# A fused attention kernel whose first batch is reordered: products ahead of masks, smaller array tiles, a shorter decoding

## The chip, the cores and the metric

The kernel runs on one core of one Trainium2 chip. The metric is the device time of the program in microseconds (us). The core's engines work side by side, each in the order of its own instructions: TensorE (PE for its products, PEld for its loads of stationary operands), VectorE (DVE), ScalarE (ACT), GpSimd (POOL) and SyncE (SP), which here only issues DMAs. They meet through semaphores alone, so an instruction that waits holds back everything behind it on its own engine.

## The reference

Two blocks follow each other. The first is a polynomial attention without softmax: queries and keys (4 batches, 4 heads, 1088 positions, 32 numbers) are turned into 64 features each, as products of two 8-number sketches. The second is a mixture of four causal attention experts, of which every position uses two.

```python
def phi(x):                                   # S1, S2: 8 x 32
    a = einsum('rd,bhsd->bhsr', S1, x);  b = einsum('rd,bhsd->bhsr', S2, x)
    return einsum('bhsi,bhsj->bhsij', a, b).reshape(..., 64)
kv  = einsum('bhsf,bhsd->bhfd', phi(k), v);   z = sum(phi(k), axis=2)
x   = einsum('bhsf,bhfd->bhsd', phi(q), kv) / (einsum('bhsf,bhf->bhs', phi(q), z) + 1e-6)
x   = x as (batch, 1088, 4 heads * 32 = 128)
logits = x @ w_gate                           # 4 experts
topk   = the two largest;  w = softmax over these two
for e in range(4):
    scores = (x @ wq[e]) @ (x @ wk[e]).T / 8, causal
    ye     = softmax(scores) @ (x @ wv[e]) @ wo[e]
    out   += w[e] * ye   where e is one of the two of the position
```

## The kernel before

The positions of a batch are cut into nine tiles of 128 (the last holds 64). Since every position uses two of four experts, each tile has two "slots" instead of four experts. The work on a batch is cut into tasks, and all tasks of the four batches are written out in one list, `ORDER` (lines 22 to 40). A word such as `0.cu:4` means: batch 0, task `cu`, argument 4. `TASKS` (line 773) maps the names to functions, and a loop at the end calls them one after the other; each call appends instructions to the engines that it uses. So the list fixes the order on every engine, the DMA queue of SyncE included. Nothing is reordered later.

The tasks that matter here, in the order of one batch:

- `ld` (`load_next`): the DMAs of k, q and v of a batch into `kin`, `qin`, `vin`, each a single buffer. `bk` (`begin_k`) copies v into `vp` on GpSimd and transposes k into `kT` on VectorE; `bq` does q. For batch 0, `vk` copies v.
- `ks`, `qs` (`sketch`, and `first_sketch` for batch 0): TensorE multiplies with the sketch matrix, ScalarE copies, VectorE and GpSimd form the 64 features. The sketch matrix itself comes in as 64-bit numbers, which VectorE decodes into a leading and a trailing fp32 part (lines 197 to 235). `SKH` is its arrangement for batch 0, `SKW` for the others.
- `kv` (`kvs`): the sums over the keys, 9 tiles x 4 heads of products whose stationary operand is a head's 64 features, into `kvz`.
- `tf` turns q's features, `nu` (`numer`) multiplies them with `kvz` and divides; the result is `xs`. `tx` turns it into `xT`. `sw` saves `xs` to DRAM, and `sp` (`spread_x`) loads it again, arranged by keys in blocks of 32, into the four row groups of the single buffer `xrep`.
- `ga`, `ge`, `gw` (`gate`): logits, choice (`sel`) and weights. `md` sends the choice through DRAM to all partitions, as masks `mk`. Batch 0 does not wait for that: `mp` (`masks`) multiplies the choice with an identity on TensorE (line 543) and has ScalarE copy it out as 8-bit masks.
- `cu` (`chosen`): for two tiles, the queries times the four experts' matrices `mcat` (line 556), then ScalarE copies two of them and VectorE puts the other two in where the mask says so (`copy_predicated`, line 562). The result `uT` holds the chosen slots. `em` makes `mcat`, `eo` the matrices of the outputs.
- `s` (scores and softmax, lines 595, 570, 574), `t` (transposition of the weights into the store of their group, `aTB` or `aTA`), `vb` and `va` (values of the two groups, line 651), `shb`, `sha`, `shp` (shares), `zb` and `o` (outputs, lines 724 to 736).
- `warm` is a task of filler products on TensorE that compute nothing.

PSUM has eight banks, and the helper `bank(n)` hands out the least recently used one or aligned group. The masks for the causal rows (`mask`, `mask_back`, `mask_last`) and other constants are built by GpSimd ahead of all tasks (lines 172 to 195).

Of the kernel before, what the change touches and what calls it, by code (L numbers as in the profile page):

```python
# [10 lines left out]
F32 = mybir.dt.float32  # L11
# [11 lines left out]
    0.bk 0.bq1 0.bq0 0.ks:0:4 0.vk 0.ks:4:9 0.qs:4:9 0.qs:0:4 0.tf:13:18 0.kv 0.eo 1.ld 0.tf:8:13 1.bk 0.tf:0:8  # L23
    1.ks:4:9 1.ks:0:4 0.nu:0:4 0.warm:2 0.nu:4:9 0.sw 0.tx:0:4 0.warm:2 1.bq 2.ld 0.warm:2 0.warm:2 0.ga:0:4 0.tx:4:9
    0.ge:0 0.gw:0 1.kv 0.ga:4:9 1.qs:4:9 0.em 0.mp:2:4 0.mp:4:6 1.tf:8:13 1.tf:13:18 0.mp:0:2 0.ge:4 0.sp 0.mp:6:8
    2.bk 0.mp:8:9 1.qs:0:4 2.bq 3.ld 1.nu:5:9 0.cu:4 0.cu:6 0.cu:0 0.gw:4 1.tf:0:8 2.ks:4:9 0.cu:2 0.s:5:1 1.nu:0:5
    2.ks:0:4 0.s:3 0.md 0.s:4:2 0.t:3 1.tx:0:4 0.t:5 0.t:1 2.kv 0.shb 1.tx:4:9 2.qs:4:9 2.qs:0:4 0.cu:8 0.s:7 0.s:8
    0.t:2 2.tf:13:18 0.t:4 1.ga:0:9 1.md 0.t:7 0.s:6:0 0.t:8 0.t:0 0.vb:0 0.vb:1 0.vb:2 0.vb:3 1.ge:0 2.tf:8:13 0.zb:3
    1.sw 1.cu:0 0.t:6 1.cu:4 0.o:3 1.cu:2 1.cu:6 1.s:4:2 0.zb:5 1.s:5:1 1.s:3 0.va:0 0.sha 3.bk 0.va:1 0.va:2 1.t:4
    1.t:5 2.tf:0:8 1.t:2 3.ks:0:4 3.bq 0.va:3 1.sp 1.t:1 2.nu:0:5 0.o:5 0.zb:6 1.cu:8 1.s:7 0.o:6 0.zb:0 2.tx:0:4  # L30
    1.t:3 3.ks:4:9 2.nu:5:9 1.s:6:0 0.zb:1 0.o:0 2.tx:4:9 1.s:8 1.gw:0 1.shb 0.zb:8 3.kv 2.ga:0:9 2.ge:0 1.vb:0 2.md
    2.sw 0.o:8 1.t:7 1.vb:1 3.qs:4:9 1.t:8 3.qs:0:4 1.t:0 1.t:6 1.vb:2 1.vb:3 2.cu:4 2.cu:2 0.o:1 1.zb:5 2.cu:0
    2.s:4:2 2.s:5:1 3.tf:13:18 1.sha 1.zb:3 1.va:0 1.va:1 3.tf:8:13 2.t:4 2.cu:6 1.o:3 1.o:5 2.t:1 3.tf:0:8 2.gw:0
    1.va:2 1.zb:1 2.t:5 1.va:3 3.nu:5:9 2.sp 2.s:3 2.t:2 2.s:6:0 3.nu:0:5 1.o:1 2.shb 2.t:3 3.sw 3.tx:4:9 1.zb:8
    3.tx:0:4 2.s:7 2.t:0 2.cu:8 1.o:8 3.ga:0:9 1.zb:6 1.zb:0 3.md 2.t:7 2.vb:0 2.vb:1 2.s:8 2.vb:2 2.vb:3 1.o:0 3.ge:0
    2.t:6 2.t:8 3.cu:8 3.cu:2 3.cu:4 1.o:6 2.sha 3.cu:0 3.cu:6 3.s:4:2 2.zb:5 3.s:5:1 3.t:2 3.t:1 3.s:3 2.zb:1 3.t:4
    3.t:3 2.o:5 2.zb:3 2.va:0 2.va:1 3.t:5 2.va:2 2.va:3 3.sp 3.s:8 2.o:3 2.o:1 3.gw:0 3.shb 3.t:8 2.zb:0 2.zb:6 3.s:7
    3.s:6:0 3.t:6 2.o:6 2.o:0 3.t:7 3.vb:0 3.vb:1 3.vb:2 3.t:0 3.vb:3 3.zb:1 3.va:0 3.va:1 3.va:2 3.zb:3 3.o:3 3.o:1
    3.shp 3.zb:5 2.zb:8 3.va:3 3.o:5 3.zb:0 2.o:8 3.o:0 3.zb:6 0.warm:2 3.zb:8 3.o:6 3.o:8
# [4 lines left out]
def kernel(  # L44
# [65 lines left out]
    kvz = const("kvz", [128, 2, D + 1])  # L110
# [60 lines left out]
    identb = const("identb", [128, 128], BF16)  # L171
    make_identity(nc, ident)
# [7 lines left out]
    for t in (mask, mask_back, mask_last):  # L180
        nc.gpsimd.memset(t, 0.0)
    for out_, cols, base in ((mask[:, 896:], 128, 0), (mask_last[0:64], 64, 0), (mask_last[64:], 64, 0),
                             *((mask_back[32 * r : 32 * r + 32, 384:], 128, 96 - 32 * r) for r in range(4))):
        nc.gpsimd.affine_select(out=out_, in_=out_, compare_op=ALU.is_ge, fill=-1e30,
                                base=base, pattern=[[-1, cols]], channel_multiplier=1)
    lower = const("lower", [128, E, E])
    nc.gpsimd.memset(lower, 0.0)
    for e in range(1, E):
        nc.gpsimd.memset(lower[:, e, 0:e], 1.0)
    nc.gpsimd.memset(SKH, 0.0)  # L190
    nc.gpsimd.memset(SKW, 0.0)
# [5 lines left out]
    if NS == 2:  # L197
# [4 lines left out]
        lead, last, ok = (words[:, x].bitcast(F32) for x in range(4, 7))  # L202
# [10 lines left out]
        def both(o, x, y, op):  # L213
# [17 lines left out]
            out=last, in0=last, scalar=2.0**-52, in1=sg.bitcast(F32), op0=ALU.mult, op1=ALU.mult)  # L231
        both(lead, ma.bitcast(F32), ok, ALU.mult)
        both(S_hi, lead, last, ALU.add)
        both(lead, lead, S_hi, ALU.subtract)
        both(S_lo, lead, last, ALU.add)
# [6 lines left out]
    for h in range(H):  # L242
        nc.gpsimd.tensor_copy(SKW[32 * h : 32 * h + 32, :, :, h % 2, :],
                              ST[:, :, 0 : 2 * R].rearrange("d n (x r) -> d n x r", x=2))
# [44 lines left out]
    def spread_x(b):  # L289
        for r in range(4):  # L290
            nc.sync.dma_start(out=xrep[32 * r : 32 * r + 32], in_=saved[b].rearrange("(c k) d -> k c d", k=32))
# [15 lines left out]
    class Batch:  # L307
# [5 lines left out]
        def __init__(self, b):  # L313
            self.b, self.ab, self.fp, self.uT, self.mp = b, {}, {}, {}, None
            self.yT, self.qpT = yT, qpT
# [17 lines left out]
    def begin_k(b):  # L333
        if b:
            nc.gpsimd.tensor_copy(vp[:, 0 : NJ - 1, :, 0:D].rearrange("p j h d -> p h j d"), vin)
            nc.gpsimd.tensor_copy(vp[0:64, NJ - 1, :, 0:D], vtl)
        n = NJ - 1
        nc.vector.transpose(kT[:, 0 : 128 * n].rearrange("p (j g t) -> p j g t", j=n, g=4),
                            kin[:, 0 : 128 * n].rearrange("p (g j d) -> p j g d", g=4, j=n))
        nc.vector.transpose(kT[:, 128 * n : S], kin[:, 128 * n : S])  # L340
# [5 lines left out]

    def load_next(b):
        load_rows(kin, k, b)
        load_rows(qin, q, b)
        load_v(b)  # L350
# [5 lines left out]
    def first_sketch(nm, j0, j1):  # L356
# [60 lines left out]
    def kvs(b):  # L417
        kp, k0 = batch(b).fp["k"], bank()
        kv = P[:, k0, 0 : 2 * (D + 1)].rearrange("p (m d) -> p m d", m=2)
        for m in range(2):  # L420
            for j in range(NJ):
                for x in range(2):
                    h = 2 * m + x
                    nc.tensor.matmul(kv[64 * x : 64 * x + 64, m], kp[:, j, h], vp[:, j, h, :],  # L424
                                     start=(j == 0), stop=(j == NJ - 1))
        nc.scalar.copy(kvz, kv)
# [6 lines left out]
    def numer(b, x0, x1):  # L433
        k0, m, qpT = bank(2), 2 * (x1 - x0), batch(b).qpT
        for y in range(2 * x0, 2 * x1):
            c = (D + 1) * (y - 2 * x0)
            for x in range(2):
                for half in (0, 64):
                    rows = slice(64 * x, 64 * x + 64)
                    nc.tensor.matmul(P[half : half + 64, k0 + x, c : c + D + 1], qpT[rows, y, half : half + 64],  # L440
                                     kvz[rows, y % 2], start=True, stop=True)
        den = p2.tile([128, 2, 2 * NJ], F32, tag="den", name=f"den{b}_{x0}")[:, :, 0:m]
        nus = P[:, k0 : k0 + 2, 0 : m * (D + 1)].rearrange("p x (m d) -> p x m d", d=D + 1)
        nc.vector.tensor_scalar_add(den, nus[:, :, :, D], 1e-6)
        nc.vector.reciprocal(den, den)
        for x in range(2):
            nc.vector.tensor_tensor(
                out=xs[:, x0:x1].rearrange("p j (m x d) -> p x (j m) d", m=2, x=2)[:, x], in0=nus[:, x, :, 0:D],
                in1=den[:, x, :, None].to_broadcast([128, m, D]), op=ALU.mult)
# [84 lines left out]
    def masks(b, j0, j1):  # L534

        m_, k0 = batch(b), bank(2)
        if m_.mp is None:
            m_.mp = p2.tile([128, NJ, 4, 128], F8, tag="mk", name=f"mp{b}")
        sb = p2.tile([128, 2, 2 * X], BF16, tag="selb", name=f"selb{b}_{j0}")
        nc.vector.tensor_copy(sb[:, 0 : j1 - j0].rearrange("p j x -> p (j x)"), m_.sel[:, 2 * X * j0 : 2 * X * j1])  # L540
        for j in range(j0, j1):
            for n, x in enumerate((1, 2, 3, 4)):
                nc.tensor.matmul(P[:, k0 + j - j0, 128 * n : 128 * n + 128],
                                 sb[:, j - j0, x : x + 1].to_broadcast([128, 128]), identb, start=True, stop=True)
        nc.scalar.copy(m_.mp[:, j0:j1].rearrange("p j x q -> p (j x q)"), flat[:, 512 * k0 : 512 * (k0 + j1 - j0)], saturate=False)

    def chosen(b, i):

# [272 lines left out]
```

## Time and profile before

| | us |
|---|---|
| median of 3 runs | 286.47 |
| lowest, highest | 284.15, 287.38 |
| profiled execution | 287.48 |
| its span, first to last instruction | 285.7 |
| TensorE busy | 272.0 |
| VectorE busy | 220.4 |
| ScalarE busy | 105.2 |
| GpSimd busy | 59.3 |
| mean granted TensorE clock | 0.982 |

The page divides the span into 40 slices of 7.14 us; a digit gives the busy share of an engine in a slice in tenths, and the row PEclk the granted clock in the same way. A row of the timeline has start, duration, engine, line, operation and tiles, with the number of merged instructions after the x; the bracket names the idle time just before it and what ended it. The chain of work that ended last is followed back from the last instruction; a piece of it has start, duration, engine, tile, line and count. A product in fp32 shows as two instructions.

### The profile page before, as it was taken

The page shows a single profiled execution, that of the slowest core. Times are in us where ns is not written, and L with a number is a line of the kernel's source. Part 1 is how long each engine was busy: PE and PEld are TensorE (multiplying, and loading weights), DVE is VectorE, ACT ScalarE, POOL GpSimd, SP SyncE. Part 2 cuts the span into 40 slices and gives each one's busy share as a digit, 9 for nine tenths or more (in the row PEclk, how much of TensorE's full clock was granted, in tenths as well). Part 3 has the DMA queues.
Part 4 walks back from the last instruction along what each step waited for, and adds up shares of the span by engine and source line. Part 5 has one row for each costly group of instructions (what it writes and reads, how often), then busy time and mean ns, then how long its engine had stood idle before and what let it go on. Part 6 is the DMA issues. An engine that isn't in the chain of part 4 may idle for free.

```text
span 285.7 us, 10500 instructions
## 1 busy us (share of the span) xinstructions
PE 272.0 (95%) x4521; PEld 218.3 (76%) x4521; DVE 220.4 (77%) x499; ACT 105.2 (37%) x262; POOL 59.3 (21%) x143
## 2 busy tenths in 40 slices
PE   7789699999999999999999999999999999999993
PEld 2776588756599769877797699678796797589983
DVE  5916859888788988988594968885988997986541
ACT  2242373384533282055212542353133622250110
POOL 8516052323311002221460021003001001000100
PEclk9979959999999999999999999999999999999999
DMA  6930999803415002692157032994433108923011
GB/s 211 266 71 22 286 184 193 187 7 126 96 31 177 21 0 71 125 181 48 33 94 196 8 49 50 164 165 97 105 122 66 22 11 156 181 52 91 12 39 38
DMA packets 41086, 28.94 MB, mean 101 GB/s; under 512 B 7504, under 2 KB 39504, under 8 KB 41040
## 3 DMA queue, kind: packets, MB, share of 16 engines
q1 hardware_dynamic: 41024, 28.28, 45.9%
q8 instruction: 35, 0.57, 0.9%
q14 instruction: 11, 0.09, 0.1%
q10 hardware_dynamic: 16, 0.00, 0.0%
HBM read 23.66 MB, written 4.60 MB: 99 GB/s over the span
## 4 chain that ended last, share of the span: by engine, by line
PE 78%; DVE 11%; DMA 4%; issue 2%; POOL 2%; ACT 0%; SPq 0%; POOLq 0%; DVEq 0%; ACTq 0%
PE P L651 23%; PE P L595 22%; PE P L733 10%; PE P L556 9%; PE P L440 3%; PE P L299 3%; PE P L401 2%; PE P L617 2%; DMA mk<-dm 2%; PE P L424 2%; DVE qT L344 2%; DMA dm<-sel 1%; DVE zT L726 1%; DVE a L570 1%; POOL qp L411 1%
## 5 line engine op out<-in xcount | busy, mean ns | idle before, releaser
L574 ACT ACTIVATE a<-a,mx 128x768 f32<-128x768 f32 (+8 forms) x68 | 53.8, 791 | 67.0 <-DVE mx L570 56.7
L595 PE MATMUL P<-xT,uT 128*128 128x512 f32 (+3 forms) x192 | 64.9, 490 | 0.2
L595 PEld LDWEIGHTS P<-xT,uT 128*128 128x128 f32 x192 | 34.0, 190 | 26.4 <-issue 18.4
L651 PE MATMUL P<-aTA,xrep 32*128 32x160 f32 (+3 forms) x1080 | 39.1, 295 | 0.0
L651 PEld LDWEIGHTS P<-aTA,xrep 32*128 32x128 f32 x1080 | 37.9, 185 | 1.3 <-DVE mx L570 0.8
L733 PEld LDWEIGHTS P<-mo,zT 128*128 128x128 f32 (+1 forms) x288 | 33.9, 185 | 4.6 <-issue 1.9
L733 PE MATMUL P<-mo,zT 128*128 128x128 f32 (+1 forms) x288 | 36.6, 279 | 0.8 <-DVE zT L726 0.7
L651 PE MATMUL P<-aTB,xrep 32*128 32x320 f32 (+4 forms) x720 | 37.2, 348 | 0.0
L570 DVE CUSTOM_DVE_ANT_0 a<-P,mask 128x768 f32<-128x768 f32 (+3 forms) x32 | 32.4, 1018 | 4.4 <-PE P L595 4.0
L651 PEld LDWEIGHTS P<-aTB,xrep 32*128 32x128 f32 x720 | 33.1, 185 | 3.3 <-issue 1.0
L556 PE MATMUL P<-xT,mcat 128*128 128x256 f32 (+1 forms) x160 | 33.6, 361 | 0.0
L556 PEld LDWEIGHTS P<-xT,mcat 128*128 128x128 f32 x160 | 27.5, 190 | 3.7 <-issue 0.5
L278 DVE STREAM_TRANSPOSE aTA<-a 128x256 f32<-128x256 f32 (+4 forms) x28 | 24.4, 916 | 1.6 <-ACT a L574 1.6
L278 DVE STREAM_TRANSPOSE aTB<-a 128x1024 f32<-128x1024 f32 (+3 forms) x28 | 24.4, 910 | 0.5 <-ACT a L574 0.5
L562 DVE COPY_PREDICATED uT<-mk,P 128x512 f32<-128x512 uint8 (+1 forms) x30 | 18.5, 637 | 7.7 <-DMA mk<-dm 4.6
L736 ACT COPY ob<-P 128x256 f32<-128x256 f32 (+2 forms) x24 | 7.5, 313 | 39.6 <-PE P L733 36.3
L726 DVE COPY_PREDICATED zT<-mk,yT 128x768 f32<-128x768 uint8 (+2 forms) x24 | 18.6, 775 | 3.9 <-POOL zT L723 1.7
L724 DVE TENSOR_TENSOR zT<-yT,mk 128x768 f32<-128x768 f32 (+2 forms) x24 | 17.0, 710 | 3.0 <-PE P L733 2.9
L411 POOL TENSOR_TENSOR kp<-kab 128x1280 f32<-128x1280 f32 (+1 forms) x6 | 13.0, 2173 | 21.1 <-DVE kab L408 12.9
L558 ACT COPY uT<-P 128x512 f32<-128x512 f32 (+1 forms) x20 | 10.3, 522 | 16.3 <-PE P L556 16.2
L570 DVE CUSTOM_DVE_ANT_0 a<-P,mask_back 128x256 f32<-128x256 f32 (+3 forms) x32 | 15.2, 484 | 0.0
L411 POOL TENSOR_TENSOR qp<-qab 128x1280 f32<-128x1280 f32 (+1 forms) x6 | 12.9, 2173 | 8.5 <-DVE qab L408 5.9
(190 smaller groups left out, 298.8 us busy)
## 6 DMA issues: line engine op xcount, KB each, us to landing
xrep<-dx SPq DMA_DIRECT2D x16, 544.0 KB, 9.0
mk<-dm SPq DMA_DIRECT2D x4, 864.0 KB, 6.0
kin<-in_k_dram SPq DMA_DIRECT2D x4, 544.0 KB, 4.1
qin<-in_q_dram SPq DMA_DIRECT2D x4, 544.0 KB, 8.0
vin<-in_v_dram SPq DMA_DIRECT2D x16, 128.0 KB, 6.8
dx<-xs SPq DMA_DIRECT2D x4, 512.0 KB, 6.6
out_dram<-ob SPq DMA_DIRECT2D x64, 16.0 KB, 2.1
out_dram<-ob SPq DMA_DIRECT2D x16, 64.0 KB, 1.6
```

The lines of the kernel that those rows point to most:

```text
L278: nc.vector.transpose(t[:, 0 : c1 - c0, n - u0 : n - u0 + s].rearrange("p c s k -> p s c k"), a[:, :, 32 * c0 : 32 * c1].rearrange("p s (c ...
L411: eng.tensor_tensor(out=fp[:, j0:j1].rearrange("p j h (x y) -> p (j h) x y", y=R), in0=a_[:, 1, :, None, :].to_broadcast([128, n, R, R]), ...
L556: nc.tensor.matmul(P[:, k0 + x // 2, x % 2 * w : x % 2 * w + w], mcat[:, e], queries, start=True, stop=True)
L558: nc.scalar.copy(u.rearrange("p t s q -> p s t q"), P[:, k0, 0 : 2 * w].rearrange("p (s t q) -> p s t q", s=2, t=n))
L562: nc.vector.copy_predicated(u, mk[:, :, :, x].bitcast(U8), c[:, :, None].to_broadcast([128, n, 2, q]))
L570: nc.vector.tensor_tensor_reduce(out=dst, in0=src, in1=msk, scale=-1.0, scalar=most, op0=ALU.add, op1=ALU.min, accum_out=mx)
L574: nc.scalar.activation(out=a, in_=a, func=ACTF.Exp, bias=mx, scale=-1.0, accum_out=z)
L595: nc.tensor.matmul(flat[:, f + c : f + c + n], turned(b, i)[:, s], m_.xT[:, c - at[i] : c - at[i] + n], start=True, stop=True)
L651: nc.tensor.matmul(P[:, sums[grp][r], 32 * us[0] : 32 * len(units)], xrep[rows, c], t[rows, c - c0, us[0] - u0 :], start=(c == 0), stop=(c ...
L724: nc.vector.tensor_tensor(out=z[:, :, 0:X], in0=y[:, :, 0, None].to_broadcast([128, n, X, nq]), in1=mk[:, :, 0:X], op=ALU.mult)
L726: nc.vector.copy_predicated(z[:, :, 1:], mk[:, :, X:].bitcast(U8), y[:, :, 1, None].to_broadcast([128, n, X, nq]))
L733: nc.tensor.matmul(P[0:nq, k0, DM * t : DM * t + DM], self.zT[:, t, e], mo[:, e], start=(e == 0), stop=(e == E - 1))
```

## The change

1. **Order and pieces.** `ORDER` is new. For batch 0 the tasks `cu` and `mp` are replaced by `ca` (the products, copied out of PSUM whole) and `cb` (the masks by TensorE, and the two predicated copies straight from PSUM). `ld` becomes `lk`, `lq` and `lv`; `sp` is called once for each row group; `bk` can be called for a part of the tiles; `kv` can be called for one pair of heads.
2. **Constants** are built in the task `pc`, in two parts that stand in the order, save `SKH` and the identities.
3. **Decoding**: the leading part is stored as it is, the trailing part too, instead of being summed and separated again: three operations fewer.
4. **Batch 0's key features** are formed by VectorE and GpSimd together, as q's already are; `vk` moves from GpSimd to ScalarE.
5. **Sums over keys** use 32 features a product in batches 1 to 3. `kvz` gets a second column block with zeros in it, so that one product can take two heads.
6. **Numerators** are formed for a pair of heads in one product, with 128 rows and 66 columns.
7. **Tile 8's products** with the experts' matrices go in two halves of 64 columns.

```diff
 ORDER = """
-    0.bk 0.bq1 0.bq0 0.ks:0:4 0.vk 0.ks:4:9 0.qs:4:9 0.qs:0:4 0.tf:13:18 0.kv 0.eo 1.ld 0.tf:8:13 1.bk 0.tf:0:8
-    1.ks:4:9 1.ks:0:4 0.nu:0:4 0.warm:2 0.nu:4:9 0.sw 0.tx:0:4 0.warm:2 1.bq 2.ld 0.warm:2 0.warm:2 0.ga:0:4 0.tx:4:9
-    0.ge:0 0.gw:0 1.kv 0.ga:4:9 1.qs:4:9 0.em 0.mp:2:4 0.mp:4:6 1.tf:8:13 1.tf:13:18 0.mp:0:2 0.ge:4 0.sp 0.mp:6:8
-    2.bk 0.mp:8:9 1.qs:0:4 2.bq 3.ld 1.nu:5:9 0.cu:4 0.cu:6 0.cu:0 0.gw:4 1.tf:0:8 2.ks:4:9 0.cu:2 0.s:5:1 1.nu:0:5
...
+    0.bk:0:4 0.bk:4:9 0.ks:0:4 0.warm:2 0.vk 0.warm:2 0.pc:0 0.bq1 0.bq0 1.lk 0.ks:4:9 0.qs:0:4 1.lv 0.warm:2 0.qs:4:9
+    0.pc:1 1.lq 0.em 0.tf:8:13 0.tf:13:18 0.kv 0.tf:0:8 1.bk 0.nu:4:9 0.eo 1.bq 1.ks:0:4 0.tx:4:9 1.ks:4:9 0.nu:0:4
+    0.ga:4:9 0.ca:8 0.ca:6 0.tx:0:4 1.kv:1:2 0.ge:4 1.kv:0:1 0.cb:8 0.gw:4 2.lv 2.lk 2.bk 0.ca:2 0.ga:0:4 2.lq
+    1.qs:4:9 0.sw 0.sp:3 0.ca:0 0.cb:0 0.sp:1 1.qs:0:4 0.sp:0 0.ca:4 0.cb:2 1.tf:13:18 3.lk 1.tf:8:13 1.tf:0:8 0.ge:0
+    0.cb:4 0.gw:0 2.ks:4:9 2.ks:0:4 2.bq 1.nu:4:9 0.s:4:2 0.s:5:1 1.tx:4:9 3.lv 0.sp:2 1.nu:0:4 2.kv:0:1 2.kv:1:2
+    0.cb:6 0.t:4 2.qs:0:4 1.sw 0.s:3 0.t:2 0.t:1 3.lq 2.qs:4:9 1.tx:0:4 0.md 0.s:7 0.t:5 2.tf:0:8 0.s:8 0.t:3 0.shb
...
+    2.sp:3 2.shb 3.tx:4:9 2.s:6:0 1.zb:1 1.o:6 2.t:2 1.zb:3 3.ga:0:9 3.md 2.t:8 3.ge:0 2.s:7 2.vb:0 2.vb:1 2.vb:2
...
 """
         nc.vector.scalar_tensor_tensor(
-            out=last, in0=last, scalar=2.0**-52, in1=sg.bitcast(F32), op0=ALU.mult, op1=ALU.mult)
-        both(lead, ma.bitcast(F32), ok, ALU.mult)
-        both(S_hi, lead, last, ALU.add)
-        both(lead, lead, S_hi, ALU.subtract)
-        both(S_lo, lead, last, ALU.add)
+            out=S_lo, in0=last, scalar=2.0**-52, in1=sg.bitcast(F32), op0=ALU.mult, op1=ALU.mult)
+        both(S_hi, ma.bitcast(F32), ok, ALU.mult)
...
+    def constants(part):
+        if part == 0:
+            nc.gpsimd.memset(SKW, 0.0)
+            nc.gpsimd.memset(kvz, 0.0)
+            ... SKW's four copies, and lower
+        else:
+            ... mask, mask_back, mask_last: three memsets, seven affine_selects
...
-    def spread_x(b):
-        for r in range(4):
-            nc.sync.dma_start(out=xrep[32 * r : 32 * r + 32], in_=saved[b].rearrange("(c k) d -> k c d", k=32))
+    def spread_x(b, r):
+        nc.sync.dma_start(out=xrep[32 * r : 32 * r + 32], in_=saved[b].rearrange("(c k) d -> k c d", k=32))
...
-        todo = [(nc.vector, second, 0, n)]
-        if nm == "q":
-            ...
+        half = spare("B", NJ * H * R * (R + int(nm == "k")), NJ * H * R).rearrange("p (j h r) -> p j h r", h=H, r=R)[:, j0:j1]
+        nc.scalar.copy(half[:, n - n // 2 :], second[:, n - n // 2 :])
+        for eng, t, x0, x1 in ((nc.vector, second, 0, n - n // 2), (nc.gpsimd, half, n - n // 2, n)):
...
-    def kvs(b):
+    def kvs(b, m0=0, m1=2):
+        kp, k0, w = batch(b).fp["k"], bank(), 32 if b else 64
...
-                for x in range(2):
-                    h = 2 * m + x
-                    nc.tensor.matmul(kv[64 * x : 64 * x + 64, m], kp[:, j, h], vp[:, j, h, :],
+                for x in range(0, 128, w):
+                    h = 2 * m + x // 64
+                    nc.tensor.matmul(kv[x : x + w, m], kp[:, j, h, x % 64 : x % 64 + w], vp[:, j, h, :],
                                      start=(j == 0), stop=(j == NJ - 1))
-        nc.scalar.copy(kvz, kv)
+        for x in range(2):
+            nc.scalar.copy(kvz[64 * x : 64 * x + 64, m0:m1, x], kv[64 * x : 64 * x + 64, m0:m1])
...
     def numer(b, x0, x1):
-        for y in range(2 * x0, 2 * x1):
-            for x in range(2):
-                for half in (0, 64):
-                    rows = slice(64 * x, 64 * x + 64)
-                    nc.tensor.matmul(P[half : half + 64, k0 + x, c : c + D + 1], qpT[rows, y, half : half + 64],
-                                     kvz[rows, y % 2], start=True, stop=True)
+        for y in range(2 * n):
+            for half in (0, 64):
+                nc.tensor.matmul(nus[half : half + 64, y // n, y % n].rearrange("p x d -> p (x d)"), qpT[:, y0 + y, half : half + 64],
+                                 kvz[:, (y0 + y) % 2].rearrange("p x d -> p (x d)"), start=True, stop=True)
...
-    def masks(b, j0, j1):
...
+    def chosen(b, i, part=None):
+        w, dw = n * q, min(128, n * q)
+        if part != 1:
+            k0 = bank(2)
...
+            for x, e in enumerate((0, E - 1, 1, 2)):
+                for d in range(0, DM, dw):
+                    nc.tensor.matmul(P[d : d + dw, k0 + x // 2, x % 2 * w : x % 2 * w + w], mcat[:, e, d : d + dw], queries,
+                                     start=True, stop=True)
             u = m_.uT[i] = ...
             nc.scalar.copy(u..., P[:, k0, ...])
+            c = P[:, k0 + 1, 0 : 2 * w]
+            if part == 0:
+                m_.first[i] = spare("B", NJ * H * R * (R + 2) + 256 * i, 2 * w)
+                nc.scalar.copy(m_.first[i], c)
+                return
+            mk = m_.mk[:, i : i + n, 1:5].bitcast(U8)
+        else:
+            k1, u, c = bank(2), m_.uT[i], m_.first[i]
+            sb = p2.tile([128, 2, 2 * X], BF16, tag="selb", name=f"selb{b}_{i}")
+            nc.vector.tensor_copy(sb..., m_.sel[:, 2 * X * i : 2 * X * (i + n)])
+            for t in range(n):
+                for y, x in enumerate((1, 2, 3, 4)):
+                    nc.tensor.matmul(P[:, k1 + t, 128 * y : 128 * y + 128],
+                                     sb[:, t, x : x + 1].to_broadcast([128, 128]), identb, start=True, stop=True)
+            mk = P[:, k1 : k1 + n].rearrange("p t (x q) -> p t x q", x=4).bitcast(I32)
         for x in range(2):
+            nc.vector.copy_predicated(u, mk[:, :, :, x], c[:, x * w : x * w + w]...)
...
     def values_of_k(b):
-        nc.gpsimd.tensor_copy(vp[:, 0 : NJ - 1, :, 0:D].rearrange("p j h d -> p h j d"), vin)
-        nc.gpsimd.tensor_copy(vp[0:64, NJ - 1, :, 0:D], vtl)
+        nc.scalar.copy(vp[:, 0 : NJ - 1, :, 0:D].rearrange("p j h d -> p h j d"), vin)
+        nc.scalar.copy(vp[0:64, NJ - 1, :, 0:D], vtl)
```

## The prediction

> **What bounds the kernel now.** I read the page first (engine shares, the 40 slices), then busy time by stretch, then the timeline of the first 80 us, and last the chain for full-speed prices of single groups.
>
> ```profile
> span 285.7 us, 10500 instructions
> PE 272.0 (95%) x4521; PEld 218.3 (76%) x4521; DVE 220.4 (77%) x499; ACT 105.2 (37%) x262; POOL 59.3 (21%) x143
> ...
> PE   7789699999999999999999999999999999999993
> ...
> DVE  5916859888788988988594968885988997986541
> ...
> PEclk9979959999999999999999999999999999999999
> ```
>
> TensorE is the bound: its row reads 9 from the sixth slice to the last but one. So the time is its useful work plus what is lost ahead of about 43 us and in the last 11. VectorE is next, mostly 8 to 9 in the middle. The stretches size the loss:
>
> ```profile
> 0.00:10.00 10.00, 7.24 (x79) 4.17 (x80) 7.08 (x28) 1.97 (x4) 6.80 (x33) 1.00 0.82 206
> 10.00:20.00 10.00, 7.80 (x197) 7.31 (x193) 5.20 (x7) 3.21 (x10) 4.19 (x6) 0.89 0.69 185
> 20.00:30.00 10.00, 9.30 (x344) 7.51 (x340) 6.22 (x17) 3.68 (x9) 4.35 (x3) 0.94 0.18 56
> 30.00:43.40 13.40, 9.97 (x269) 8.72 (x265) 8.48 (x38) 8.10 (x18) 4.06 (x5) 0.75 1.09 229
> 43.40:60.00 16.60, 16.60 (x219) 12.41 (x220) 15.27 (x41) 7.02 (x17) 5.30 (x5) 1.00 0.82 158
> ```
>
> Columns: stretch, length, busy PE, PEld, DVE, ACT, POOL, then clock. At 43.4 us the first batch's `chosen` begins and TensorE never rests again. Until then it is busy 34.3 of 43.4 us. Idle: 9.1. Filler multiplications: 5.1 (the first four) and 2.1 (eight of `warm`), 7.2. In two-microsecond stretches the clock reads 0.50 to 0.72 from 18 to 22 us and again from 34 to 42 us, which costs 4.2 to 4.7. So 21.0 of the 43.4 us are lost and 22.4 are useful work. The last idle of the head is this one:
>
> ```profile
> 9.53 1.05 POOL L756 COPY vp<-vin 128x1024 f32<-128x1024 f32 x1 [1.81 <-DMA vin<-in_v_dram]
> ...
> 10.06 2.37 PE L370 MATMUL P<-aTA,qT 128*64 128x64 f32 x72
> ...
> 35.64 1.89 PE L543 MATMUL P<-identb,selb 128*128 128x128 bf16 x16 [1.99 <-DVE selb L540]
> ...
> 73.89 0.78 PE L476 MATMUL P<-wg,xT 128*32 128x4 f32 x72
> ```
>
> L543 (the masks) waits 2 us for VectorE, which came through the batch-1 transposition (2.2 us), two gate chains (1.9 us each) and the cast.
>
> **Part 1, array tiles, at full clock.** The prices, from the chain (start, us, what, count):
>
> ```profile
> 42.46 0.91 PE P L440 x64
> 55.50 1.30 PE P L440 x80
> 63.05 2.22 PE P L424 x72
> 118.55 0.84 PE P L556 x8
> ```
>
> An fp32 product is two instructions here. *Tile 8 of `chosen`*: 8 instructions of 128x128 take 0.84 us. Afterwards 16 of 128x64 with 64 moving columns, the form of L370 (2.37/72 = 33 ns): 0.53. Saved 0.31 x 4 batches = 1.25. *Numerators*: 144 of 64x64 (0.91 + 1.30 = 2.21 us) become 72 of 128x64 with 66 columns, again L370's form: 2.37. Lost 0.16 x 4 = 0.65. *Sums over keys*, batches 1 to 3: 72 instructions of 128x64 (2.22 us) become 144 of 128x32. Two sources disagree. The nearest row is the gate, 128x32 tiles: 0.78/72 = 11 ns each; the 64x64 numerators took 15 ns with the same 33 columns. I take 12.5 ns: 1.80 us, saved 0.42 x 3 = 1.25 (ends: 0 and 2.0). [...] Sum of part 1: 1.9 us gained; with the rule, 3.4 lost.
>
> **Part 2, the head.** I walked the new order on each engine with the durations of the timeline.
> - Decoding loses three VectorE operations, 0.75 us: the sketch matrix is ready at 5.7 instead of 6.5. Half of k's transposition (0.63 of 1.25 us) lets TensorE start at 6.5 instead of 7.9. GpSimd's mask building (some 4 us) moves behind q's features, so nothing waits for it there.
> - The key features do not come sooner: ScalarE now copies v in its order, and v lands at 9.5 (row L756). Its copy of 1.3 us ends at 10.8, so the second half of the k products runs on VectorE and GpSimd from 11.2 to 12.4, against 12.46 before. The split in two engines saves 1.2 us of VectorE only.
> - q's sketches end at 13.6; the experts' matrices and turned features run to 16.3, sums over keys to 18.5, first numerators to 20.5. Batch 1's q transposition (2.2 us of VectorE) lies ahead of the second numerators' division, which ends at 26.4.
> - `ca` offers 7.5 us of TensorE work (0.53 + 4 x 1.73) that waits for no mask. Products of tiles 8 and 6 run at 24.9 to 27.2. Then batch 1's key sums wait for GpSimd's features (1.95 + 2.39 us from 24.7) until 29.0: 1.5 idle. `ca:2` and `ca:0` cover most of the second gate chain; `cb:0` still waits 1.8 for VectorE, 0.35 more goes for GpSimd's q features.
> - The first scores (`0.s:4:2`) start at 45.9, with 31.8 us useful work done (22.4 and 9.4 more: 7.5 of `ca`, the rest batches 1 and 2). Lost by then, summed: 6.5 at the start, 1.5 filler, 0.9 (q), 0.95 (ScalarE's copies), 0.55, 1.5, 1.8, 0.35 = 14.05.
>
> Added: 0.8 for `cb:6`, whose cast is queued on VectorE behind scores and a division, and 2.0 for the clock. [...] But here it fell at 18 us after 14 to 18 with 2.75 us busy and no gap over 0.8. So I book one such fall (half of four microseconds). Lost: 16.85 against 21.0, a gain of 4.15. [...]
>
> **Part 3, what should cost nothing.** ScalarE loses five mask copies (about 1 us each), gains five of products (0.59, one 0.27) and some copies of sums (0.2 each); it is 37% busy, so the PE hides it, save that a late sum delays numerators by 0.2, covered by 0.6 us of turned features. `copy_predicated` now takes a four-byte mask from PSUM: 0.74 us by L562 (1.45 ns an element; L726 has 1.34 with all in SBUF), at worst doubled, 6 us of VectorE in the stretch where it is fullest. I take 0.74. xrep's spread is cut into four DMAs of 544 KB: SyncE needs 2.1 us for each, landing took 9.0 in a group of four and 4.1 for the same bytes of k. In batch 2 the last piece has 9.8 us of TensorE work ahead of its values; needed 2.1 + 4.1, at worst 11.1: 0 to 1.3 us, I take 0. Batch 2's loads stand ahead of the first batch's save on SyncE, but their buffers are free (24.1) before xs is written (26.4). The tail keeps its chain: last values, yT, two zT, two outputs; the two fillers dropped there lay in a gap.
>
> **Sum.** 4.15 + 1.9 = 6.05 us. The profiled execution, 287.48 (span 285.7 and 1.8 around it), would become 281.4; from the median of the runs, 286.47, it is 280.4.
>
> **Rivals.**
> - *Head gain lost, tile gain stays.* Two clock falls more (2 us each) or v landing late eat the 4.15. For it: two falls before, half-busy stretches remain from 6 to 20 us. Against: `ca` fills the second place. 286.47 - 1.9 = 284.6.
> - *Everything fills.* No fall, the rest of the casts in time, key sums at 11 ns: 6.95 + 2.7 = 9.6, so 276.9.
> - *Slower: VectorE holds the casts.* Each `cb` makes TensorE, in order, wait for a 0.24 us cast queued on VectorE behind transpositions (1.45, 2.2), divisions (1.3) and sketch additions (0.5). VectorE is busy 15.3 of 16.6 us from 43.4 on, and in the old kernel L543 waited for just this cast. The price is five waits; it turns the sign from 1.2 us each beyond my walk, and at 2.0 each (a doubled predicated copy would do) it loses 10: 290.4. Against: the casts I walked were mostly ready, and a wait at one lets VectorE catch up for the next.
>
> A measurement of this kernel tells about 1% from no change.
>
> **How the numbers follow.** Forecast 0.53 (277.5 to 283.5), everything fills 0.12, head gain lost 0.18, slower 0.17. Faster by over 1% (under 283.6): 0.53 + 0.12 + 0.04 of the lost-head case = 0.69; within: 0.14; slower: 0.17. The range goes from 275.5 (no idle beyond the walk, key sums at the low end) to 289.0, which takes in the lost head with the worst of part 3 and leaves out most of the slower case.
>
> **What would show it.** [...] I am wrong if TensorE shows gaps after 50 us, or if casts lead its waits.

## The result and the profile after

| | before | after |
|---|---|---|
| median, us (20 runs each) | 286.61 | 284.63 |
| lowest, highest | 284.07, 289.76 | 282.91, 285.60 |
| profiled execution | 287.48 | 285.60 |
| its span | 285.7 | 283.7 |
| mean granted TensorE clock | 0.982 | 0.991 |

The ratio of the times is 0.9937, interval 0.9912 to 0.9962: 2.0 us faster, a third of the forecast 6.05. Executions fall into a fast and a slow state; all ratios here compare fast ones alone. From the page of the changed kernel: its span, busy shares, two of the rows in 40 slices with the clock, and from section 3 the queue that carries instructions (packets, MB, share of 16 DMA engines).

```profile
span 283.7 us, 10439 instructions
...
PE 268.5 (95%) x4477; PEld 212.3 (75%) x4477; DVE 218.8 (77%) x497; ACT 107.3 (38%) x276; POOL 59.1 (21%) x144
...
PE   8899699979999999999999999999999999999983
...
DVE  5639577989789989888677886797988889988260
...
PEclk9999899999999999999999999999999999999998
...
q8 instruction: 35, 0.57, 0.9%
```

The PE row fills up one slice sooner than before, and then, as before, has a 6 in its fifth slice (28 to 35 us). The clock reads 8 there, where before it read 9. Busy time by stretch shows the same place (columns as in the prediction; the last two columns are the DMA share and GB/s):

```profile
0.00:10.00 10.00, 8.89 (x75) 4.58 (x77) 5.29 (x25) 2.08 (x5) 3.07 (x17) 1.00 0.72 192
10.00:20.00 10.00, 8.33 (x221) 7.29 (x219) 5.35 (x7) 5.19 (x16) 7.73 (x23) 1.00 0.72 199
20.00:30.00 10.00, 9.39 (x310) 7.98 (x310) 8.46 (x16) 5.79 (x14) 5.46 (x5) 1.00 0.57 162
30.00:43.40 13.40, 10.06 (x232) 8.20 (x219) 8.30 (x38) 4.48 (x16) 4.03 (x5) 0.87 0.87 168
43.40:60.00 16.60, 15.83 (x378) 11.87 (x376) 13.88 (x43) 8.89 (x23) 6.65 (x5) 1.00 0.56 111
...
28.00:30.00 2.00, 2.00 (x85) 1.47 (x85) 1.93 (x2) 1.66 (x3) 1.64 (x2) 1.00 0.99 319
30.00:32.00 2.00, 0.31 (x35) 0.20 (x21) 1.45 (x10) 0.59 (x4) 0.00 (x0) 1.00 0.95 292
32.00:34.00 2.00, 0.92 (x59) 0.92 (x59) 0.00 (x0) 0.00 (x0) 0.00 (x0) 0.74 0.11 31
34.00:36.00 2.00, 2.00 (x19) 1.67 (x10) 1.04 (x6) 0.36 (x2) 0.00 (x0) 0.50 0.44 124
```

From 30 to 34 us TensorE is busy 1.23 of 4 us, no other engine has anything to do between 32 and 34, and the DMA engines run at 0.95 to 0.99 until 32. The clock falls right behind it. In the timeline, PE and one ScalarE row:

```profile
6.97 1.20 PE L370 MATMUL P<-aTA,kT 128*64 128x64 f32 x32
...
10.50 1.07 ACT L759 COPY vp<-vin 128x1024 f32<-128x1024 f32 x1 [1.91 <-DMA vin<-in_v_dram]
...
29.22 1.09 PE L422 MATMUL P<-vp,kp 128*32 128x33 f32 x85
33.08 1.09 PE L422 MATMUL P<-vp,kp 128*32 128x33 f32 x59 [2.77 <-issue]
...
49.62 7.16 PE L598 MATMUL P<-xT,uT 128*128 128x512 f32 x24
...
58.26 1.46 PE L422 MATMUL P<-vp,kp 128*32 128x33 f32 x144
60.87 0.62 PE L559 MATMUL P<-identb,selb 128*128 128x128 bf16 x8 [1.16 <-DVE selb L556]
...
109.98 0.98 PE L437 MATMUL P<-kvz,qpT 128*64 128x66 f32 x26 [0.33 <-issue]
...
134.88 8.57 PE L654 MATMUL P<-aTB,xrep 32*128 32x320 f32 x176 [0.61 <-issue]
```

Batch 1's sums over keys stop after 85 of 144 products for 2.77 us. Their operands are the same tiles as those of the 85 before. The bracket says "issue": no engine and no data transfer released it. The first scores start at 49.62; in the kernel before they start here:

```profile
51.89 3.61 PE L595 MATMUL P<-xT,uT 128*128 128x512 f32 x12
```

TensorE's longest waits in the changed kernel (total, times, longest):

```profile
PE P L422 <- issue: 2.8, 1, 2.8
PE P L559 <- DVE selb L556: 1.9, 3, 1.2
```

So the longest wait is one that no step of the prediction has.

### The profile page after: what moved, and what is told of

It is laid out like the page before. It is cut to its first block, busy times and chain, and to the rows that moved or that the text cites. A ratio compares the mean times of both kernels' runs of the same rounds, so it can differ in the third digit from the quotient of the medians.

```text
span 283.7 us, 10439 instructions
## 1 busy us (share of the span) xinstructions
PE 268.5 (95%) x4477; PEld 212.3 (75%) x4477; DVE 218.8 (77%) x497; ACT 107.3 (38%) x276; POOL 59.1 (21%) x144
## 4 chain that ended last, share of the span: by engine, by line
PE 81%; DVE 7%; issue 4%; ACT 3%; POOL 2%; SPq 2%; DMA 1%; ACTq 0%; POOLq 0%; DVEq 0%
PE P L654 27%; PE P L598 20%; PE P L736 10%; PE P L543 9%; PE P L620 3%; DVE qT L349 2%; PE P L302 2%; PE P L437 2%; PE P L162 2%; ACT a L577 2%; PE P L398 2%; POOL kp L408 2%; SPq L744 1%; PE P L370 1%; PE P L422 1%
## 5 line engine op out<-in xcount | busy, mean ns | idle before, releaser
L577 ACT ACTIVATE a<-a,mx 128x128 f32<-128x128 f32 (+7 forms) x68 | 53.7, 791 | 49.7 <-DVE mx L573 49.4
L573 DVE CUSTOM_DVE_ANT_0 a<-P,mask 128x640 f32<-128x640 f32 (+3 forms) x32 | 32.3, 1017 | 2.6 <-PE P L598 1.4
L543 PEld LDWEIGHTS P<-xT,mcat 128*128 128x128 f32 (+1 forms) x192 | 26.4, 176 | 3.8 <-issue 0.3
L282 DVE STREAM_TRANSPOSE aTB<-a 128x1024 f32<-128x1024 f32 (+3 forms) x28 | 25.0, 922 | 1.5 <-ACT a L577 1.3
L408 POOL TENSOR_TENSOR kp<-kab 128x1024 f32<-128x1024 f32 (+1 forms) x6 | 12.9, 2172 | 19.1 <-DVE kab L405 19.1
L573 DVE CUSTOM_DVE_ANT_0 a<-P,mask_back 128x384 f32<-128x384 f32 (+3 forms) x32 | 15.1, 485 | 0.0
```

What stands on the lines that cost most here:

```text
L282: nc.vector.transpose(t[:, 0 : c1 - c0, n - u0 : n - u0 + s].rearrange("p c s k -> p s c k"), a[:, :, 32 * c0 : 32 * c1].rearrange("p s (c ...
L408: eng.tensor_tensor(out=fp[:, j0:j1].rearrange("p j h (x y) -> p (j h) x y", y=R), in0=a_[:, 1, :, None, :].to_broadcast([128, n, R, R]), ...
L543: nc.tensor.matmul(P[d : d + dw, k0 + x // 2, x % 2 * w : x % 2 * w + w], mcat[:, e, d : d + dw], queries, start=True, stop=True)
L573: nc.vector.tensor_tensor_reduce(out=dst, in0=src, in1=msk, scale=-1.0, scalar=most, op0=ALU.add, op1=ALU.min, accum_out=mx)
L577: nc.scalar.activation(out=a, in_=a, func=ACTF.Exp, bias=mx, scale=-1.0, accum_out=z)
```

## What the old trace already said

In the timeline of the kernel before, two rows carry the same releaser:

```profile
16.61 0.54 PE L424 MATMUL P<-vp,kp 128*64 128x33 f32 x11 [0.78 <-issue]
...
25.31 0.42 PE L440 MATMUL P<-kvz,qpT 64*64 64x33 f32 x12 [0.70 <-issue]
```

Counting products from the start, 223 stand before the first gap and 478 before the second: 255 apart, which is twice 128 within the records that a trace loses. In the changed kernel the 85th product of batch 1's sums is number 605 of the program, 127 further. The page counts a load for every product (PE x4477, PEld x4477), so 128 products are 256 instructions. The `q8` line gives the rest: 35 packets, 0.57 MB, so 16 KB each; and 2 x 4477 instructions divided by 35 packets is 256. The number of packets went with TensorE's count: 34 with 4405 products (e2_sums64), 37 with 4765 (e4_numer). **TensorE's own instructions come in by DMA, in blocks of 256**, and the page counts the time of their packets on the same 16 DMA engines as the data's. The trace keeps each packet of this queue with its time. In the changed kernel the packet of the block behind product 605 runs from 30.82 to 31.80 us, and the sums go on at 33.08.

*Theory:* every 128 products TensorE goes on with the next block, and waits where that isn't there yet. From entering a block to using the next took 3.4 us with the DMA engines almost idle (before: block entered at 21.9, packet from 22.58 to 23.92, next block in use at 25.3; DMA share 0.00 to 0.08 from 22 to 26 us), and 7.0 us beside the burst of loads (after: 26.07 to 33.08). By estimate from the row at 58.26 (144 products in 1.46 us, 10 ns each) a block of them is used up in 1.3 us, less than either, so a burst of small products runs dry, and most where loads are on their way. *Rivals:* the gap is a late operand which the trace misnames; the loss lies in the new tail; the casts are what costs.

## Experiments, first set

The kernel before stands at 287.77 us beside these.

**e1_loads: batch 2's k and q loads moved behind the first transfer of x; `2.bk` follows them, and batch 3's k load (`3.lk`) moves down two words.**

```diff
-0.gw:4 2.lv 2.lk 2.bk 0.ca:2 0.ga:0:4 2.lq 1.qs:4:9 0.sw 0.sp:3 0.ca:0 0.cb:0 0.sp:1
+0.gw:4 2.lv 0.ca:2 0.ga:0:4 1.qs:4:9 0.sw 0.sp:3 2.lk 0.ca:0 0.cb:0 2.lq 0.sp:1
-1.tf:13:18 3.lk 1.tf:8:13 1.tf:0:8 0.ge:0 0.cb:4 0.gw:0
+1.tf:13:18 2.bk 1.tf:8:13 1.tf:0:8 0.ge:0 0.cb:4 0.gw:0 3.lk
```

> Changed kernel with batch 2's loads of k and q issued behind the first piece of 0's spread, and 2.bk behind the casts of cb:0 and cb:2; nothing else. Late instructions theory: TensorE's own instructions come by DMA in blocks of about 128 products (35 packets, 0.57 MB, for 4477 products), and the block that ends the 2.8 us gap inside batch 1's sums over keys (30.3 to 33.1 us) stood behind 1.7 MB of loads. Then the gap falls under 0.7 us, the clock stays at 1.00 from 32 to 37 us, the first scores start at 45.5 to 47.5 instead of 49.6, and the time falls by 2.5 to 4 us. Hidden semaphore theory: the second half of the sums waits for something on ScalarE or GpSimd; the gap stays at 2.5 us or more, time within 0.7 us. VectorE theory (the casts hold TensorE anyway): the gap goes but the waits for selb grow from 1.9 to 4 us or more, time within 1 us.

Measured: 282.80 us, ratio 0.9825 (0.9786 to 0.9865), clock 1.0, first scores at 46.98, no gap in batch 1's sums. That is 1.9 us under e3_tail below, which on the same chip changes only the end; 2.5 to 4 were expected. The casts cost more, not less: 3.5 us in four waits against 1.9.

```profile
PE P L558 <- DVE selb L555: 3.5, 4, 1.4
```

So the gap's 2.8 us came back, or nearly, although the casts got worse. From the first scores to the end it takes 233.9 us, against 234.1 in the changed kernel: the whole gain lies ahead of them.

**e2_sums64: batch 1 sums over keys by 64 features again** (`32 if b > 1 else 64`).

> Changed kernel with 64 features a product in batch 1's sums, 32 only in batches 2 and 3. Late instructions theory: 72 products fewer, so the block's border moves out of the sums to the gate of tiles 0 to 3, which TensorE reaches at about 33.8 us, after the block is there (33.1): no gap over 0.7 us, no half clock; the sums cost 0.8 us more; net 1 to 3 us faster. Hidden semaphore theory: the gap stays in the second half, net 0.5 to 1 us slower. VectorE theory: the gap goes, casts wait longer, time within 1 us.

Measured: 285.84 us, ratio 0.9938 (0.9903 to 0.9973): no faster than the change, a miss. In the timeline of this kernel the gap has left the sums of batch 1 and turned up in batch 2's gate:

```profile
30.01 2.29 PE L422 MATMUL P<-vp,kp 128*64 128x33 f32 x72
...
132.49 0.67 PE L472 MATMUL P<-wg,xT 128*32 128x4 f32 x42 [2.52 <-issue]
```

72 products fewer shift every later block border by 72 products, and one of them now falls behind batch 3's 144 quick sums. The sums of batch 1, now without a border inside, run through: their operands were not what was late. In this run a border wasn't removed, only moved, and it cost 2.52 us in the new place.

**e3_tail: in batch 3 the outputs of tiles 1 and 3 stand earlier, that of tile 5 later.**

```diff
-3.va:0 3.zb:5 3.zb:1 3.va:1 3.o:5 3.shp 3.o:1 3.zb:3 3.va:2 3.va:3 3.o:3 3.zb:0
+3.va:0 3.zb:1 3.zb:3 3.va:1 3.o:1 3.shp 3.va:2 3.o:3 3.zb:5 3.va:3 3.o:5 3.zb:0
```

> Changed kernel with the outputs of tiles 3 and 4 of batch 3 put ahead of the last part of the values, tile 5's output as filler behind it. Output queue theory: from the last product to the end of the span it takes 4.8 us (3.6 before), as SyncE issues the eight DMAs of tiles 3 and 4 in the tail and ob's two buffers come free late; then that drops to 3.6 to 3.9 and the time falls by 0.8 to 1.3 us. Rival: the tail is set by the chain yT, zT, products alone; the 4.8 stays, time within 0.4 us.

Measured: 284.71 us, ratio 0.9925 (0.9886 to 0.9964). The stretch from the last product to the end fell from 4.8 to 3.2 us as expected, but TensorE now waits 0.80 us for VectorE's `zT` ahead of it. From the first scores to the end: 234.28 us against 234.08. The tail theory falls.

**e4_numer: the old form of the numerators, 64 rows and one head each** (144 products a batch for 72).

> Changed kernel with the numerators as before (144 instructions of 64x64 with 33 columns a batch, heads in two banks). By prices alone: 2.2 instead of 2.4 us a batch, up to 0.6 us faster. Late instructions theory: 72 more instruction pairs before batch 1's sums (numerators of batch 0), so the border of the late block comes 72 pairs earlier in the stream, around the gate and tile 8's products at 25 to 27 us; the gap moves there or shrinks, and every batch has more blocks to fetch: between 0.6 faster and 2 us slower. Hidden semaphore theory: the gap stays in the second half of batch 1's sums.

Measured: 288.25 us, ratio 1.0027 (0.9989 to 1.0066), 0.9% above the changed kernel's 0.9937. At most 2 us slower was expected, so this is a miss. By its rows the old form is 0.04 us a batch cheaper (batch 3: 1.37 + 1.14 us against 1.39 + 1.16), not 0.16. Waits of TensorE in this kernel:

```profile
PE P L422 <- issue: 3.7, 2, 2.6
PE P L657 <- issue: 2.0, 2, 1.8
PE P L398 <- issue: 1.3, 1, 1.3
```

Seven us of "issue" against 3.7 in the changed kernel, and the gap in batch 1's sums now stands behind the 141st product, number 733: one block on from 605. A gap in the second half of these sums was the sign of the hidden semaphore too, so its place alone settles nothing here; its number, and e2_sums64, do. Numerators by pairs pay, though not by their own time: they halve the instructions.

## Experiments, second set

The kernel before stands at 286.94 us. The changed kernel itself was run again beside them (a_after, the unchanged text).

> The changed kernel itself, as measure for the runs beside it on the same chip. Late instructions theory: a gap with nothing to wait for behind the 85th of 144 products of batch 1's sums again (605 products from the start), 1.5 to 3 us long, first scores at 48 to 50 us; 0.992 to 0.996 of before.

Measured: 282.90 us, ratio 0.9881 (0.9837 to 0.9926). In its timeline:

```profile
30.43 0.72 PE L422 MATMUL P<-vp,kp 128*32 128x33 f32 x59 [0.20 <-issue]
...
46.61 4.58 PE L598 MATMUL P<-xT,uT 128*128 128x512 f32 x14
```

The same program, the same border before product 86, but a gap of 0.20 us where 1.5 to 3 were expected. The three profiled executions of the changed kernel (b_after comes below):

| execution | gap at product 605 | first scores | span |
|---|---|---|---|
| a_after | 0.20 | 46.61 | 280.9 |
| b_after | 1.81 | 47.91 | 282.6 |
| after (the first profile) | 2.77 | 49.62 | 283.7 |

2.57 us more gap went with 3.0 us at the first scores (0.3 of them there from the first sketch on) and 2.8 us of span, the fall of the clock included. In these profiles the gap goes with the chip: f3_decode, on the chip of a_after, has 0.19, and g2_extra, on that of b_after, 1.68. In a_after SyncE issued batch 2's k load at 23.31 us, in the first profile of the changed kernel at 25.14, so the burst ended sooner (30.4 for 32 us).

**f1_casts: e1_loads, and two VectorE steps moved about the casts of `cb:4` and `cb:6`.**

```diff
-1.tf:13:18 2.bk 1.tf:8:13 1.tf:0:8 0.ge:0 0.cb:4 0.gw:0 3.lk
+1.tf:13:18 1.tf:8:13 1.tf:0:8 0.ge:0 0.cb:4 2.bk 0.gw:0 3.lk
-2.kv:0:1 2.kv:1:2 0.cb:6 0.t:4 2.qs:0:4 1.sw
+2.kv:0:1 2.kv:1:2 2.qs:0:4 0.cb:6 0.t:4 1.sw
```

> As e1_loads, with 2.bk behind cb:4's cast and predicated copies, and 2.qs:0:4 ahead of cb:6. Late instructions theory with the casts as what came next: no gap in batch 1's sums, the waits for selb fall from 3.5 to 1.5 us or less, first scores at 45.3 to 46.5, 0.5 to 1.5 us faster than e1_loads, 0.977 to 0.980 of before. Rival (VectorE is the bound in this stretch, each wait that goes comes back at the next product that needs it): waits move to the scores or values, no faster than e1_loads (0.9825).

Measured: 286.44 us, ratio 0.9993 (0.9966 to 1.0021): the whole gain gone, a miss. Casts waited less (2.2 us in four), but batch 2's key sketches stood behind a transposition that was now late:

```profile
45.82 2.20 PE L397 MATMUL P<-SKW,kT 64*64 64x64 f32 x72 [2.86 <-DVE kT L344]
```

First scores at 50.34. Here the slower rival of the prediction shows itself in another place: VectorE's queue does bind once its steps stand wrong; in the change they don't.

**f2_tiles: the kernel before, with its old order, and only the new array tiles** (sums over keys by 32, numerators by pairs, tile 8 in halves).

> The kernel before with the array tiles of the change alone (sums by 32 features in batches 1 to 3, numerators by pairs, tile 8 in halves), in the old order. By prices: three batches of sums 0.76 us, four tiles 0.33, numerators 0.2 dearer: 2.8 us, of which about 1 lies in the head under other waits: 1.8 to 2.8 us faster. Late instructions theory: the border at 605 products now lies behind about the 131st of 144 products of batch 1's sums, reached at 29 to 30 us, and its block is asked for at about 28 us, together with batch 2's loads: a gap of 2 to 5 us there with nothing to wait for; TensorE waits until 35.6 for the masks anyway, so 0 to 2 us of the gain are left.

Measured: 288.16 us, ratio 1.0039 (1.0004 to 1.0074): slightly slower, where part 1 of the prediction books 1.9 us of gain. Waits of TensorE in it:

```profile
PE P L426 <- issue: 2.5, 1, 2.5
PE P L476 <- issue: 2.2, 1, 2.2
PE P L300 <- issue: 1.4, 1, 1.4
...
PE P L402 <- issue: 1.2, 1, 1.2
```

7.7 us of "issue" in all against 1.5 in the kernel before. The first stands before the 132nd product of batch 1's sums, behind number 605 again, as the count of blocks had said:

```profile
29.56 0.29 PE L426 MATMUL P<-vp,kp 128*32 128x33 f32 x11 [2.55 <-issue]
```

The span grew by only 0.7 (286.4 for 285.7), so the products did get cheaper, or other waits were swallowed; but the gain went into waiting for instructions.

**f3_decode: the changed kernel with the three decoding operations back.**

> The changed kernel with the three decoding operations back. Prediction's step: they cost 0.75 us of VectorE, first sketch 0.75 us later. Rival: VectorE then waits 0.84 us for k (landed at 5.83) in the changed kernel, so the decoding is hidden: first sketch within 0.2 us of 6.97, time within 0.5 us of the changed kernel.

Measured: 282.95 us, ratio 0.9900 (0.9844 to 0.9956), beside 282.90 for the changed kernel. First sketch at 6.68 us against 6.65. The decoding was hidden: without the three operations VectorE waits 0.46 us for k to land (0.84 in the first profile of the changed kernel), and with them it works in that time.

## Experiments, third set

The kernel before stands at 286.48 us, the changed kernel (b_after) at 284.61, ratio 0.9971 (0.9943 to 0.9999).

> The changed kernel itself again, as measure on the same chip. So far its gap in batch 1's sums over keys was 2.8, 1.8, 0.2 and 0.2 us in four profiles of the same head, and ended each time within 1.1 us of the end of the burst of loads (32, 31, 30.5, 31 us). Late instructions theory: again the gap ends within about 1 us of the end of the burst, whatever its length.

So it came, in its timeline:

```profile
31.41 1.03 PE L422 MATMUL P<-vp,kp 128*32 128x33 f32 x59 [1.81 <-issue]
...
47.91 7.16 PE L598 MATMUL P<-xT,uT 128*128 128x512 f32 x24
```

The burst ended at about 30.4 us: the DMA share is 1.05 from 28 to 30 us, 0.43 in the next us and 0.07 in the one after.

**g1_late_q: only batch 2's q load moved,** behind `0.sp:3`.

```diff
-0.ga:0:4 2.lq 1.qs:4:9 0.sw 0.sp:3 0.ca:0
+0.ga:0:4 1.qs:4:9 0.sw 0.sp:3 2.lq 0.ca:0
```

> The changed kernel with batch 2's load of q alone issued behind the first piece of 0's spread (k and v stay where they were, and 2.bk too). Late instructions theory: the burst is 0.56 MB shorter, some 2 us, and ends before 30 us; no gap over 0.3 us behind the 85th product of the sums, no clock fall at 32 to 37 us, first scores at 46 to 47 in every profile; 1 to 2.5 us faster than the changed kernel beside it. If the load doesn't set the gap (it only varies from chip to chip): no change beyond 0.7 us.

Measured: 282.69 us, ratio 0.9890 (0.9851 to 0.9928). That is 1.9 us under the changed kernel beside it. One DMA of 544 KB less in the burst, and there is no "issue" gap in the sums; first scores at 46.96.

```profile
28.91 0.46 PE L421 MATMUL P<-vp,kp 128*32 128x33 f32 x32
29.68 1.19 PE L421 MATMUL P<-vp,kp 128*32 128x33 f32 x112 [0.31 <-POOL kp L407]
```

**g2_extra: nothing but DMA traffic added:** batch 3's k, v and q are loaded a second time, at a place where no load was.

```diff
-0.t:0 0.sha 1.s:4:2
+0.t:0 0.sha 3.lk 3.lv 3.lq 1.s:4:2
```

> The changed kernel with three more loads (k, v and q of batch 3 once more, 1.64 MB, into buffers whose contents are used up, or get the same contents) behind the first batch's shares, at about 100 us; no other instruction changes. At 107 us the changed kernel had a gap of 0.3 to 0.6 us in the numerators of batch 2, at a border 128 products after the last. Late instructions theory, with the DMA load as what makes a block late: the gap grows to 2 to 4 us, and the time by 1.5 to 3.5. If the rate alone sets it (a block takes 3.3 us whatever the load): the gap stays under 0.8 us, the time within 0.5 us.

Measured: 288.04 us over twelve executions; the eight that its ratio counts have a median of 287.41, 2.8 over the changed kernel's 284.61 beside it. Ratio to before 1.0023 (0.9976 to 1.0069). The profiled execution, 289.40, is not among the eight, so its rows are read for the gap and not for the time. One row of its timeline, then its counterpart in b_after:

```profile
112.24 1.70 PE L436 MATMUL P<-kvz,qpT 128*64 128x66 f32 x26 [3.94 <-issue]
```

```profile
108.20 0.98 PE L437 MATMUL P<-kvz,qpT 128*64 128x66 f32 x26 [0.31 <-issue]
```

and busy time by stretch, first of g2_extra, then of b_after:

```profile
106.00:109.00 3.00, 2.30 (x67) 1.99 (x63) 2.86 (x6) 0.27 (x1) 0.00 (x0) 1.00 0.99 252
109.00:112.00 3.00, 0.00 (x0) 0.00 (x0) 1.78 (x4) 0.00 (x0) 0.00 (x0) 1.00 1.14 185
```

```profile
106.00:109.00 3.00, 2.69 (x80) 2.38 (x76) 2.97 (x6) 0.27 (x1) 0.00 (x0) 1.00 0.01 2
109.00:112.00 3.00, 3.00 (x100) 2.93 (x96) 2.61 (x7) 0.00 (x0) 0.00 (x0) 1.00 0.02 5
```

The border before the last 26 numerators of that half costs 0.31 us in b_after, where the DMA share (last column but one) is near zero from 106 us on. With 1.6 MB of loads beside it, it costs 3.94. At product 605, ahead of the added loads, the gap is 1.68, much as in b_after (1.81). TensorE's instructions and all its operands are the same. That is the decisive run: with nothing but loads added, the packet for this border starts at 109.21 and not at 105.91 us (table below). The transfer of instructions is what waits, and data transfers hold it up.

**g3_loads: e1_loads again,** beside the changed kernel.

> e1_loads again, beside the changed kernel on the same chip. No gap in batch 1's sums; first scores at 46.8 to 47.2; as fast as the changed kernel where that has its short gap, up to 2 us faster where it has its long one; slower than g1_late_q by 0.3 to 1 us, since 2.bk then stands ahead of a cast (1.4 us wait).

Measured: 282.45 us, ratio 0.9882 (0.9834 to 0.9929), against 0.9971 (0.9943 to 0.9999) for the changed kernel: the intervals don't meet. It was expected 0.3 to 1 us behind g1_late_q (282.69) and is level with it. From its page and its timeline:

```profile
PEclk9999999999999999999999999999999999999999
```

```profile
29.05 1.46 PE L421 MATMUL P<-vp,kp 128*32 128x33 f32 x144
...
46.44 4.79 PE L597 MATMUL P<-xT,uT 128*128 128x512 f32 x15
```

All 144 sums in one piece, the first scores 1.5 us sooner than in b_after (3.2 sooner than in the profile after), and no fall of the clock. It beats both kernels, by three loads and one step on VectorE written further down in a list.

**The packets themselves.** The traces say when each block came. Times in us; "entered" is when the first product of the block before started:

| run, border behind product | entered | packet | next product | gap |
|---|---|---|---|---|
| after, 605 | 26.07 | 30.82 to 31.80 | 33.08 | 2.77 |
| b_after, 605 | 25.49 | 29.16 to 30.09 | 31.41 | 1.81 |
| a_after, 605 | 26.14 | 27.99 to 29.00 | 30.43 | 0.20 |
| g1_late_q, 605 | 25.78 | 27.85 to 28.82 | 30.15 | none |
| b_after, 1880 | 103.25 | 105.91 to 106.83 | 108.20 | 0.31 |
| g2_extra, 1880 | 103.66 | 109.21 to 110.63 | 112.24 | 3.94 |

The packet itself takes 0.9 to 1.4 us in these rows, and the next product follows 1.3 to 1.6 us behind it. What the loads stretch is mostly the time until it starts. The same holds for all 49 "issue" gaps of TensorE in the fourteen profiles: each stands at a border (within the records that a trace loses), and each ends 1.2 to 1.7 us after a packet of this queue has landed. So the rival of a late operand that the trace misnames is out. What decides the place of the packet among the loads isn't shown: in a_after it ran inside the burst, in the first profile near its end.

## Why the prediction was right or wrong

**The step that failed** is part 2's walk of the head. It let TensorE wait for semaphores alone and put the wait for its own instructions at nothing; the opening's sentence that engines meet through semaphores alone leaves the same wait out. In its place stood the block border at product 605: 2.77 us, and behind it the half clock from 32.9 to 36.4 us. With the border nearly free and the clock at 1.00 up to the first scores (a_after) these start at 46.61; the walk has 45.9, and 47.9 with the 2.0 booked for the clock. With the border they start at 49.62. The span of a_after, 280.9, is 4.8 us under that of before, so most of the forecast is there when the border costs little. The trace of before showed two such gaps of 0.7 to 0.8 us, and the prediction passes over them.

**The rest of the shortfall.** In profile terms the forecast was 281.4 and the execution took 285.6: 4.2 us, 4.1 of them inside the span. 1.7 lie ahead of the first scores, as said. The other 2.4 lie behind them: 234.1 us where the sum leaves 231.7. Rows account for this much: waits at and behind `cb:6` 1.16 and 0.35 where 0.8 was booked (0.7); the borders at 109.98 and 134.88 (0.9); the stretch after the last values 12.1 us for 11.3 (0.8), though e3_tail shows that this isn't to be had by its order; against them the sums of batches 2 and 3, cheaper by 0.34 each. Together 1.7; the last 0.7 us stay open.

**Part 1.** The prices of single products were close or too high: numerators 1.32 + 1.09 = 2.41 us a batch between starts (2.37 forecast), tile 8's products 0.52 to 0.66 in batches 1 to 3 (0.53), sums 1.46 (1.80), predicated copies 1.51 for two, 0.76 each (0.74). No run shows the "rule" by which the sum of part 1 has 3.4 us lost; the row held: 144 products in 1.46 us are 10.1 ns each. But the sum of prices was not the gain: f2_tiles has the tiles alone at 1.0039. The 10.1 ns hold no wait for instructions. By estimate from the 3.4 us of the kernel before, a block every 3.4 us would be 27 ns a product for as long as that goes on; no run here holds that rate. So the three changes together gained nothing (f2_tiles), by way of the supply (7.7 us of "issue" against 1.5) and not of a product's own time. One sum of the prediction is slightly off: key sums at 11 ns give 2.5 us gained in the best case, not 2.7.

**Part 2, single steps.** The copy of v ended at 11.6 and not at 10.8, since v landed a us later. The first sketch came at 6.97 for 6.5, since k landed at 5.83; that the shorter decoding would bring 0.75 us was wrong (f3_decode). The idle 1.5 us before batch 1's key sums did not come. `cb:0` waited 0.56 and not 1.8, as the gap covered the rest (a_after, nearly without the gap, waits 1.42 there). The casts' longest wait, 1.16, is under 2 us: the slower rival did not happen. One fall of the clock was booked in the head, and one came, but behind the gap; a_after has none there. That count came out by luck.

**Signs named in advance.** "Gaps after 50 us": there were, small ones (0.33 and 0.61 of "issue"). "Casts lead its waits": no, second to "issue". **Rivals.** The time came out at the "head gain lost, tile gain stays" figure (284.6), but by luck: the tiles alone gain nothing (f2_tiles), so what stayed is rather a part of the order's gain.

## What to carry to other kernels

Count a kernel's TensorE products in blocks of 128 and look where the borders fall (the gaps of the changed kernel stand at 605, 1880 and 2390): an idle PE with "issue" as its releaser at such a number was, in all 49 cases of these profiles, waiting for its own instructions. A price from the trace is not yet a gain where smaller products need more instructions: the small tiles alone came out at 1.0039 (f2_tiles). Fewer instructions paid here though each product costs more (batch 3's numerators: 72 in 2.55 us, before 144 in 2.51): ratio 0.9937 with pairs, 1.0027 without (e4_numer). Look for bursts of loads beside a border that lies in quick products: 1.6 MB of loads took one from 0.31 to 3.94 us (g2_extra), and one load of 544 KB moved away took another from 1.81 us to none (g1_late_q).

## What the runs showed of the hardware

- TensorE's instructions came in packets of 16 KB, 256 instructions each (after: 35 packets, 0.57 MB, 4477 products with as many loads). The first eight packets of the changed kernel start between about 1 us before and 5.9 us after the block before is entered. How many blocks are held ahead wasn't shown.
- From entering a block to using the next it took 3.4 us on almost idle DMA engines (before, 21.9 to 25.3 us); beside loads the gap went from 0.31 to 3.94 us at one and the same border (b_after, g2_extra).
- The same program shows gaps of 0.20, 1.81 and 2.77 us at the same product in three executions, and spans of 280.9, 282.6 and 283.7. The longer the gap, the longer the span; how much of the spread between chips this is wasn't shown.
- The clock was halved (0.50) for 3.4 us behind gaps of 2.77 us (after, from 32.9 us on) and of 1.81 us (b_after, from 31.5). Behind gaps of 1.68 us (g2_extra) and of 0.20 us (a_after) it reads 1.00 up to 36 us. What sets it wasn't shown.
